# Storing the result of a decode kernel from ScalarE's DMA queue in place of SyncE's

## The chip, the cores and the metric

The kernel runs on one core of one Trainium2 chip. The metric is the device time of one execution in microseconds (us), and medians of several executions are quoted. The span of a profile is about 1.8 us shorter than the time on the clock, so spans are compared with spans and times with times. In the views of the profile SP is SyncE, PE TensorE, DVE VectorE, ACT ScalarE and POOL GpSimd; a q at the end of such a name marks what the engine's sequencer does, and L247 is line 247 of the kernel.

## The reference, cut to what matters

One token attends to a cache of 65,536 keys and values per head, is projected, and is mixed by a gate with the output of a small token MLP.

```python
def reference(A_x, A_k_cache, A_v_cache, A_wq, A_wo, B_x, B_w1, B_b1, B_w2, B_b2, gate_w):
    g = _sigmoid((x * gate_w).sum(-1, keepdims=True))
    # A: q = x @ wq; 16 query heads on 8 KV heads; Sk = 65536, Dh = 256
    #    softmax(q k^T * Dh**-0.5) @ v, then @ wo
    # B: layernorm, outer product with w1 + b1, gelu, sum over F with w2, + b2
    return g * a + (1 - g) * b        # shape (1, 1, 448), bf16
```

The two caches hold 2 x 8 x 65536 x 256 bf16 values, 537 MB. The result is 448 bf16 values, 896 bytes.

## The kernel before

SyncE issues all the large loads, in program order, each after a wait for its buffer to come free. At the end it also stores the result. ScalarE uses its own DMA queue for six small loads at the very start and then runs a loop of copies and exponentials.

```python
        @block.sync
        def _(eng):
            # ... wq loads ...
            for j in range(NP):                       # 32 blocks of keys and values
                last = j == NP - 1
                if j >= 1:
                    eng.wait_ge(sem_tr[NB - 1], BODY * (j - 1) + DC)   # TensorE has read the keys
                load(kring, A_k_cache, j, 0, HV if last else NV, HV * (j % 2), sem_k)
                # ...
                else:
                    eng.wait_ge(sem_pv, j)                             # TensorE has read the values
                load(vbuf, A_v_cache, j, 0, NLATE if last else NV, 0, sem_v)
                # ... the last block in pieces; wo_sb once per head ...
            eng.wait_ge(s_fin, 1)
            eng.dma_start(out_ap, out_g[0:P:P // NCG, :]).then_inc(sem_out, 16)
            eng.wait_ge(sem_out, 16)
```

The result lies in `out_g` in four partitions (0, 32, 64 and 96) of 112 values each. VectorE writes it as the last piece of work:

```python
            vec.wait_ge(s_proj, H)
            vec.scalar_tensor_tensor(out_g[:, :], prj[:, 0:WG], bcast[:, 0:1], run_g[:, :],
                                     op0=ALU.mult, op1=ALU.add).then_inc(s_fin, 1)
```

ScalarE's program ends with its loop:

```python
        @block.scalar
        def _(act):
            # ... six small loads, sqrt, exp ...
            with nc.Fori(0, NP, 1, engines=OrderedEngineSet([act.engine])) as j:
                # ... evacuations of transposed keys (ktT), exponentials (pT) ...
                with act.If(j < FT):
                    act.wait_ge(s_u, j + 1)
                    act.activation(z_b[:, :], z_b[:, :], AF.Tanh).then_inc(s_tanh, 1)
```

The softmax here doesn't subtract the row's maximum and nothing guards it: scores larger than these inputs give would overflow.

Of the kernel before, what the change touches and what calls it, by code (L numbers as in the profile page):

```python
# [12 lines left out]
def bass_gated_mix__gqa_block_cached__mixer_token_mlp__decode_kernel(  # L13
# [25 lines left out]
    P = 128  # L39
# [28 lines left out]
    NCG = 4  # L68
# [22 lines left out]
    with ctx:  # L91
        def sb(shape, dt, name):
            return ctx.enter_context(nc.sbuf_tensor(name, shape, dt))
# [4 lines left out]
        def new_sem(name):  # L98
            return ctx.enter_context(nc.semaphore(name))
# [56 lines left out]
        out_g = sb([P, WG], bf16, "out_g")  # L156
# [43 lines left out]
        s_fin = new_sem("s_fin")  # L200
        sem_out = new_sem("sem_out")
# [4 lines left out]
        out_ap = out.rearrange("a b (q n) -> (a b q) n", q=NCG)  # L206

        def src(cache, j, n0=0, n1=NV):
            g, m = divmod(j, PPH)
            s = cache[0, g, m * BODY * CH:(m + 1) * BODY * CH, :].rearrange("(p n) d -> p n d", p=P)  # L210
            return s[:, n0:n1, :].rearrange("p n d -> p (n d)")

        @block.sync
        def _(eng):
            eng.dma_start(wq_a.rearrange("p j n -> p (j n)"),  # L215
                          A_wq[0:WF * P, :].rearrange("(p j) n -> p (j n)", p=P)).then_inc(sem_wq, 16)
            eng.dma_start(wq_b, A_wq[WF * P:DM, :].rearrange("r (a n) -> (r a) n", a=2)  # L217
                          ).then_inc(sem_wq, 16)
            def load(dst, cache, j, n0, n1, at, sem):
                eng.dma_start(dst[:, at + n0:at + n1, :].rearrange("p n d -> p (n d)"), src(cache, j, n0, n1)  # L220
                              ).then_inc(sem, 16)

            for j in range(NP):
                last = j == NP - 1
                if j >= 1:
                    eng.wait_ge(sem_tr[NB - 1], BODY * (j - 1) + DC)
                load(kring, A_k_cache, j, 0, HV if last else NV, HV * (j % 2), sem_k)
                if last:
                    load(kring, A_k_cache, j, HV, NV, HV, sem_kb)
                if j == 0:  # L230
                    eng.wait_ge(s_q, 1)
                    eng.wait_ge(s_hb, 1)
                else:
                    eng.wait_ge(sem_pv, j)
                load(vbuf, A_v_cache, j, 0, NLATE if last else NV, 0, sem_v)
                if last:
                    for (n0, n1), sem in zip(pieces, sem_vp):
                        load(vbuf, A_v_cache, j, n0, n1, 0, sem)
                if j % PPH == 0:
                    g = j // PPH  # L240
                    if g >= 1:
                        eng.wait_ge(s_proj, g)
                    eng.dma_start(wo_sb[:, :, :],
                                  A_wo[g * REP * DH:(g + 1) * REP * DH, :].rearrange(
                                      "(h p j) n -> p h (j n)", h=REP, j=2)).then_inc(sem_wo, 16)
            eng.wait_ge(s_fin, 1)
            eng.dma_start(out_ap, out_g[0:P:P // NCG, :]).then_inc(sem_out, 16)  # L247
            eng.wait_ge(sem_out, 16)

        @block.gpsimd  # L250
        def _(eng):
# [10 lines left out]
        def _(pe):  # L262
# [74 lines left out]
            def piece_wait(n):  # L337
                for (n0, _), sem in zip(pieces, sem_vp):
                    if n == n0:
                        pe.wait_ge(sem, 16)  # L340
# [249 lines left out]
        @block.scalar  # L590
        def _(act):
            act.dma_start(xrow_b, x_row_ap).then_inc(sem_x, 16)
            act.dma_start(grow_b, gate_w.rearrange("(a n) -> a n", a=1)).then_inc(sem_misc, 16)
            for i, w in enumerate((B_w1.rearrange("a f -> (a f)"), B_b1, B_w2.rearrange("f a -> (f a)"))):
                act.dma_start(wrows_b[i * FT:(i + 1) * FT, :], w.rearrange("(k p) -> k p", p=P)
                              ).then_inc(sem_misc, 16)
            act.dma_start(b2_b[:, :], B_b2.rearrange("(a n) -> a n", a=1)).then_inc(sem_misc, 16)
            act.sem_inc(sem_exp, 2)
            for b in range(1, NB, 2):
                act.sem_inc(sem_ev[b], 1)  # L600
            act.wait_ge(s_d2a, 1)
            act.sqrt(statb[:, 3:4], statb[:, 2:3])
            act.activation(statb[:, 5:6], statb[:, 4:5], AF.Exp, scale=-1.0).then_inc(s_a2d, 1)

            pt_reg = act.alloc_register("pt_reg")
            act.reg_mov(pt_reg, DC)


            def weights(k, c):
                p0 = act.snap(pt_reg, min_val=0, max_val=DC)  # L610
                act.wait_ge(sem_qk, c + 3)
                act.activation(pT[:, bass.ds(p0 + k % DC, 1), :].rearrange("p o n -> p (o n)"),  # L612
                               sps[:, k % 2, 0:2 * NT], AF.Exp, scale=scale).then_inc(sem_exp, 1)
                if k == DC - 1:
                    act.reg_sub(pt_reg, DC, pt_reg)

            with nc.Fori(0, NP, 1, engines=OrderedEngineSet([act.engine])) as j:
                c0 = act.snap(j * BODY, min_val=0, max_val=NC)
                for k in range(BODY):
                    act.wait_ge(sem_qk, c0 + (k + 1))  # L620
                    for b in range(1, NB, 2):
                        act.wait_ge(sem_tr[b], c0 + (k + 1))
                        act.activation(ktT[:, k % KTB, b, :], kst_b[:, b, :], AF.Copy).then_inc(sem_ev[b], 1)  # L623
                    if k >= 1:
                        weights(k - 1, c0 + (k - 1))
                weights(BODY - 1, c0 + (BODY - 1))
                with act.If(j < FT):
                    act.wait_ge(s_u, j + 1)
                    act.activation(z_b[:, :], z_b[:, :], AF.Tanh).then_inc(s_tanh, 1)  # L629


# [26 lines left out]
```

## Time and profile before

| | before |
|---|---|
| time, median of the first 3 runs (range) | 1270.92 us (1270.15 to 1271.19) |
| span of the profile | 1268.1 us |
| bytes moved, mean rate | 544.39 MB, 429 GB/s |
| chain that ended last | DMA 68%, PE 31%, all else rounds to 0% |
| start of `out_g` to the end of the span | 2.41 us, 0.19% of the span |

The chain that ended last is the work that the profile follows back from the last instruction, at each step to what released it. The page of the kernel before has these lines on DMA and on this chain. In the queue lines, q1 is SyncE's queue, q10 is ScalarE's, and q8 and q14 fetch instructions; the columns are packets, megabytes and the share of the engines' time.

```profile
DMA packets 12366, 544.39 MB, mean 429 GB/s; under 512 B 1345, under 2 KB 3395, under 8 KB 3779
q1 hardware_dynamic: 12264, 544.22, 99.4%
q10 hardware_dynamic: 90, 0.01, 0.0%
DMA 68%; PE 31%; issue 0%; SPq 0%; DVE 0%; ACT 0%; ACTq 0%
```

The kernel is a stream of cache reads. SyncE's queue moves practically every byte, and its issuing engine rounds to 0% of the chain. What SyncE itself waits for is shown by the view of the waits of the DMA queue's own engine (waiter, releaser: us in total, times, longest):

```profile
SPq L220 <- PE kst L277: 646.5, 31, 25.2
SPq L220 <- PE acc L327: 530.2, 31, 24.4
SPq L247 <- DVE out_g L587: 31.5, 1, 31.5
SPq L91 <- DMA out_dram<-out_g: 1.0, 1, 1.0
```

SyncE waits nearly all the time for TensorE to give buffers back. Before the store (line 247) it has waited 31.5 us for VectorE, so no cache load is left for it to issue. After the store it waits 1.0 us for the data to land. That the last loads have also landed is shown by the view by windows of the 4.08 us before the store (start:end and length in us, then busy us of PE, PEld, which is TensorE's loading of weights, DVE, ACT and POOL, granted TensorE clock, DMA share, GB/s):

```profile
1261.98:1266.06 4.08, 2.59 (x86) 2.36 (x84) 1.30 (x5) 0.00 (x0) 0.00 (x0) 0.96 0.01 4
```

At 4 GB/s, against a mean of 429, no stream of loads is left for the store to queue behind.

The timeline of the end of the kernel before (start us, duration us, engine, line, operation, and in brackets the idle time before it and who ended it):

```profile
1264.97 0.16 DVE L545 TENSOR_TENSOR oTn<-sps,rden 128x4 bf16<-128x4 f32 x1 [1.96 <-PE sps L347]
1265.70 0.33 DVE L587 SCALAR_TENSOR_TENSOR out_g<-prj,bcast,run_g 128x112 bf16<-128x112 f32 x1 [0.57 <-PE prj L367]
1266.06 0.65 SPq L247 DMA_DIRECT2D out_dram<-out_g  x1
```

And the closing instructions of every engine, which share the line number 91 (engine, operation, count: duration in ns min/median/max, first and last start us):

```profile
L91 ACTq DRAIN  x1: 8/8/8, 1257.1 to 1257.1; - x1
L91 SPq COMPARE_BRANCH  x1: 33/33/33, 1267.7 to 1267.7; - x1
L91 SPq DRAIN  x1: 7/7/7, 1267.9 to 1267.9; - x1
L91 PEldq EVENT_SEMAPHORE  x1: 51/51/51, 1268.1 to 1268.1; - x1
```

ScalarE has nothing to do from 1257.1 us on. The store takes 0.65 us on SyncE's sequencer, and SyncE goes on (COMPARE_BRANCH) at 1267.7, when the data has landed. The 0.65 us alone would mislead: the Trainium skill, "Perfetto Trace Analysis", section "Summary: the profiler window per engine type", says that the record of such a DMA ends with the issue and leaves out the movement of the data. This trace agrees: the store was issued in 0.65 us, and SyncE was released 1.02 us after that record ended.

### The profile page before, as it was taken

How to read it: one execution, taken by the hardware profiler on the slowest of the kernel's cores; microseconds unless marked ns; L12 is line 12 of the kernel's file. 1: busy time of each engine (PE TensorE's matmuls, PEld its weight loads, DVE VectorE, ACT ScalarE, POOL GpSimd, SP SyncE). 2: the span in 40 equal slices, each digit the busy share in tenths (PEclk: the TensorE clock that was granted, in tenths of full speed). 3: DMA queues.
4: the chain of work that ended last, by engine and by line, in shares of the span. 5: the costliest groups of instructions: out<-in, count | busy, mean ns of one | idle time of the engine just before them, and what ended most of it. 6: DMA issues, size and time to landing. Idle time of an engine off the chain costs nothing.

```text
span 1268.1 us, 38721 instructions
## 1 busy us (share of the span) xinstructions
PE 912.6 (72%) x17053; PEld 860.7 (68%) x17055; DVE 417.9 (33%) x741; ACT 537.2 (42%) x786; POOL 0.9 (0%) x7
## 2 busy tenths in 40 slices
PE   1886668766778666697665876767867678766698
PEld 1776667766678666687665876657866568765687
DVE  2433334333344333343222332223332223331233
ACT  0543345543355433455333553334543245532355
POOL 0000000000000000000000000000000000000000
PEclk9988789788898788888788988789887788887889
DMA  9999999999999999999999999999999999999997
GB/s 411 424 428 438 432 432 428 438 436 430 436 426 438 434 430 440 426 436 432 432 440 426 436 430 436 436 428 434 430 440 432 430 432 430 442 432 430 430 424 323
DMA packets 12366, 544.39 MB, mean 429 GB/s; under 512 B 1345, under 2 KB 3395, under 8 KB 3779
## 3 DMA queue, kind: packets, MB, share of 16 engines
q1 hardware_dynamic: 12264, 544.22, 99.4%
q8 instruction: 8, 0.13, 0.0%
q10 hardware_dynamic: 90, 0.01, 0.0%
q14 instruction: 4, 0.02, 0.0%
HBM read 544.22 MB, written 0.00 MB: 429 GB/s over the span
## 4 chain that ended last, share of the span: by engine, by line
DMA 68%; PE 31%; issue 0%; SPq 0%; DVE 0%; ACT 0%; ACTq 0%
DMA kring<-in_A_k_cache_dram 68%; PE kst L277 25%; PE sps L297 5%; PE acc L327 1%; PE kst L313 0%; PE sps L347 0%; PE acc L319 0%; PE sps L354 0%; ACT pT L612 0%; SPq L217 0%; PE prj L367 0%; SPq L215 0%; DVE out_g L587 0%; DVE oTn L545 0%; ACTq L612 0%
## 5 line engine op out<-in xcount | busy, mean ns | idle before, releaser
L277 PE MATMUL kst<-ident,kring 128*128 128x128 f32 x4096 | 561.5, 298 | 314.7 <-DMA kring<-in_A_k_cache_dram 313.6
L623 ACT ACTIVATE ktT<-kst 128x1024 bf16<-128x1024 bf16 x512 | 499.5, 1021 | 671.2 <-PE kst L277 670.9
L277 PEld LDWEIGHTS kst<-ident,kring 128*128 128x128 f32 x4096 | 511.9, 155 | 324.3 <-issue 321.6
L529 DVE COPY ktT<-kst 128x1024 bf16<-128x1024 bf16 x512 | 354.1, 692 | 775.4 <-PE kst L277 751.9
L297 PEld LDWEIGHTS sps<-qcur,ktT 128*128 128x128 bf16 x8192 | 237.8, 96 | 4.6 <-issue 2.1
L297 PE MATMUL sps<-qcur,ktT 128*128 128x2 bf16 x8192 | 236.6, 163 | 1.9 <-issue 1.9
L327 PE MATMUL acc<-vbuf,pT 128*2 128x256 bf16 x4064 | 142.8, 309 | 3.1 <-issue 3.1
L327 PEld LDWEIGHTS acc<-vbuf,pT 128*2 128x2 bf16 x4064 | 104.8, 94 | 33.1 <-issue 3.9
L612 ACT ACTIVATE pT<-sps 128x32 f32 x256 | 51.8, 202 | 17.0 <-PE sps L297 17.0
L319 PE MATMUL acc<-pT,ones_sq 128*128 128x32 bf16 x256 | 11.7, 178 | 12.7 <-ACT pT L612 12.7
L319 PEld LDWEIGHTS acc<-pT,ones_sq 128*128 128x128 bf16 x256 | 8.6, 97 | 15.4 <-ACT pT L612 15.4
L629 ACT ACTIVATE z_b<-z_b 128x448 bf16<-128x448 bf16 x14 | 8.1, 577 | 20.4 <-DVE z_b L516 20.4
L534 DVE COPY accs<-acc 128x288 f32<-128x288 f32 x8 | 3.7, 458 | 37.9 <-PE acc L327 37.9
L381 PE MATMUL acc<-vbuf 42*128 42x42 bf16 x1 | 0.2, 215 | 8.5 <-DMA b_b<-in_B_b_dram 8.5
L381 PEld LDWEIGHTS acc<-vbuf 42*128 42x128 bf16 x1 | 0.1, 99 | 8.6 <-DMA b_b<-in_B_b_dram 8.6
L510 DVE TENSOR_TENSOR z_b<-wtmp,u_b 128x448 bf16<-128x448 bf16 x14 | 5.5, 393 | 1.0
L522 DVE TENSOR_TENSOR gu<-wtmp,z_b 128x448 bf16<-128x448 bf16 x14 | 5.5, 392 | 1.0
L520 DVE TENSOR_SCALAR z_b<-z_b 128x448 bf16<-128x448 bf16 x14 | 3.9, 277 | 5.9 <-ACT z_b L629 5.9
L508 DVE TENSOR_TENSOR wtmp<-u_b 128x448 bf16<-128x448 bf16 x14 | 5.5, 392 | 1.0
L514 DVE TENSOR_TENSOR z_b<-u_b,wtmp 128x448 bf16<-128x448 bf16 x14 | 5.5, 392 | 1.0
L504 DVE TENSOR_SCALAR wtmp<-hbT,params 128x448 bf16<-128x448 bf16 x14 | 4.7, 337 | 2.6 <-issue 2.6
L506 DVE TENSOR_SCALAR u_b<-wtmp,params 128x448 bf16<-128x448 bf16 x14 | 4.7, 337 | 2.6 <-issue 2.6
(84 smaller groups left out, 80.5 us busy)
## 6 DMA issues: line engine op xcount, KB each, us to landing
kring<-in_A_k_cache_dram SPq DMA_DIRECT2D x2, 4096.0 KB, 22.8
vbuf<-in_A_v_cache_dram SPq DMA_DIRECT2D x1, 6144.0 KB, 24.4
wo_sb<-in_A_wo_dram SPq DMA_DIRECT2D x8, 448.0 KB, 28.6
vbuf<-in_A_wq_dram SPq DMA_DIRECT2D x1, 3072.0 KB, 10.3
vbuf<-in_A_v_cache_dram SPq DMA_DIRECT2D x1, 1024.0 KB, 26.5
vbuf<-in_A_v_cache_dram SPq DMA_DIRECT2D x1, 768.0 KB, 27.5
vbuf<-in_A_wq_dram SPq DMA_DIRECT2D x1, 512.0 KB, 11.1
kring<-in_A_k_cache_dram SPq DMA_DIRECT2D x31, 27.8
```

The costliest lines, as they stand in the source:

```text
L277: ins = pe.transpose(kst[:, b, i * P:(i + 1) * P], kring_f[:, at + NT * (k % DC) + 4 * b + i, :], ident[:, :])
L297: ins = pe.matmul(sps[:, par, 2 * nt:2 * nt + 2], ktT[:, par, b, ntl * DH + dj:(ntl + 1) * DH:2], qcur[:, dj, :], start=(dj == 0), stop=(d ...
L319: pe.matmul(acc[:, DENC:SELC], ones_sq[:, :], pT[:, r, :], start=False, stop=(r == BODY - 1), skip_group_check=True)
L327: ins = pe.matmul(acc[o:o + REP, 0:DH], pT[:, r, 2 * nt:2 * nt + 2], vbuf[:, n, :], start=False, stop=False, skip_group_check=True)
L508: vec.tensor_tensor(W, U, U, op=ALU.mult)
L510: vec.tensor_tensor(Z, W, U, op=ALU.mult)
L514: vec.tensor_tensor(Z, U, W, op=ALU.add)
L522: vec.tensor_tensor(gu[:, :], W, Z, op=ALU.mult).then_inc(s_pb, 1)
L529: vec.tensor_copy(ktT[:, k % KTB, b, :], kst_b[:, b, :]).then_inc(sem_ev[b], 1)
L612: act.activation(pT[:, bass.ds(p0 + k % DC, 1), :].rearrange("p o n -> p (o n)"), sps[:, k % 2, 0:2 * NT], AF.Exp, scale=scale).then_inc(s ...
L623: act.activation(ktT[:, k % KTB, b, :], kst_b[:, b, :], AF.Copy).then_inc(sem_ev[b], 1)
L629: act.activation(z_b[:, :], z_b[:, :], AF.Tanh).then_inc(s_tanh, 1)
```

## The change: intent and diff

The store is issued by ScalarE, which has been idle for 9 us, rather than by SyncE, which has carried all the loads. The thought behind it is that a store on another queue can't be held up by the stream of loads.

```diff
@@ SyncE, after the loop of loads
-            eng.wait_ge(s_fin, 1)
-            eng.dma_start(out_ap, out_g[0:P:P // NCG, :]).then_inc(sem_out, 16)
-            eng.wait_ge(sem_out, 16)
@@ ScalarE, after its loop
                     act.activation(z_b[:, :], z_b[:, :], AF.Tanh).then_inc(s_tanh, 1)
+            act.wait_ge(s_fin, 1)
+            act.dma_start(out_ap, out_g[0:P:P // NCG, :]).then_inc(sem_out, 16)
+            act.wait_ge(sem_out, 16)
```

## The prediction

> **What bounds the kernel now.** It streams two caches: the page's DMA row reads 544.39 MB at a mean of 429 GB/s, and queue 1 (SyncE's) has 99.4% of the engines' time. The chain that ended last is 68% DMA (loads of `kring`) and 31% PE; SyncE's queue, VectorE and ScalarE round to 0%. SyncE's own waits are 646.5 us for TensorE to free `kring` and 530.2 us for it to free `vbuf`. A 0.9 KB store cannot change that stream.
>
> **The one stage touched** is the tail, from the timeline. VectorE starts `out_g` at 1265.70 us and takes 0.33 us. SyncE issues the store at 1266.06 (0.65 us), then waits 1.0 us for its completion, branches at 1267.7, and the closing semaphores end at 1268.1. So issue plus completion is about 1.65 us of 1268.1, 0.13%, all on the critical path.
>
> **What the change removes, adds and moves.** The listing of instruction order shows one DMA copy fewer on SyncE and one more at ScalarE's end, nothing else but line numbers. The store still waits for the same VectorE semaphore, then for its own completion.
> - No queueing is saved: SyncE's last cache loads are issued by 1234.6, and the last 4.1 us before the issue moved 4 GB/s (windows view).
> - ScalarE is free: its last activation ends at 1257.03, about 9 us before the store, so an instruction after its loop delays none of its work.
> - Issue on ScalarE: its small loads at the start took 0.21 to 0.53 us each, against 0.33 to 0.44 us for SyncE's cache loads. These overlap. My estimate from them is 0.65 us, give or take 0.2.
> - Completion: the Trainium skill, "DMA: Bandwidth & Descriptors", section "Issuing engines are not separate DMA queues", says that DMAs of either engine run on the same 16 DMA engines. So I keep 1.0 us. This trace, with its single store, cannot confirm it.
> - End: ScalarE in place of SyncE comes last to the closing barrier; their drains take 8 and 7 ns. No difference.
> - Early: ScalarE's six small loads already go through its queue (queue 10, 90 packets); the store is 1,250 us later.
>
> The sum is 0.0 us, give or take 0.3. The run-to-run range before is 1.04 us, so the change should not be visible in the time.
>
> **Prediction: 1270.9 us, 8 times in 10 between 1268.8 and 1273.0.** The range is mostly the spread between occasions, not the change. Chances: faster by over 2% 0.005, within 2% 0.99, slower by over 2% 0.005.
>
> **What would show each step right or wrong.** At the end of the timeline ScalarE's queue issues the store within 0.1 us of the end of `out_g`, for 0.45 to 0.85 us, and the last semaphore comes 1.9 to 2.3 us after that issue starts. The queue table gives queue 1 eight packets fewer (four data, four semaphores) and queue 10 eight more, 98. Bytes, GB/s and the chain's shares stay within a per cent. SyncE reaches its closing drain about 31 us earlier, and nobody profits.
>
> **What would make it wrong.** An instruction fetch after ScalarE's loop that takes longer than the 9 us of slack; a slow first use of ScalarE's queue after a millisecond of idleness; a completion from this queue that takes microseconds; or loops shifted in instruction memory so that PE or ScalarE slows in every pass, which the unchanged order makes unlikely. Any but the last costs single microseconds, far below the 25 us that 2% would take.

## The result, and the profile after

| | before | after |
|---|---|---|
| time, median of 6 runs each (range) | 1270.95 us (1270.09 to 1271.19) | 1271.14 us (1270.13 to 1271.51) |
| ratio, 95% interval | | 1.0002 (0.9989 to 1.0015) |
| span of the profile, granted clock | 1268.1 us, 0.847 | 1269.3 us, 0.842 |
| start of `out_g` to the end of the span | 2.41 us | 2.44 us |

Ratios here and below are the mean time of one kernel's fast runs over that of the other's of the same rounds, so they are not quite the ratio of the medians.

The time is the same. The page of the kernel after, same lines as before:

```profile
DMA packets 12365, 544.39 MB, mean 429 GB/s; under 512 B 1344, under 2 KB 3394, under 8 KB 3778
q1 hardware_dynamic: 12256, 544.22, 99.3%
q10 hardware_dynamic: 98, 0.01, 0.0%
DMA 68%; PE 31%; issue 0%; SPq 0%; DVE 0%; ACT 0%; ACTq 0%
```

Eight packets have moved from q1 to q10, and nothing else has: these are the four rows of the store and their four semaphore writes. The timeline of the end and the closing instructions of the kernel after:

```profile
1266.14 0.16 DVE L542 TENSOR_TENSOR oTn<-sps,rden 128x4 bf16<-128x4 f32 x1 [2.01 <-PE sps L344]
1266.87 0.33 DVE L584 SCALAR_TENSOR_TENSOR out_g<-prj,bcast,run_g 128x112 bf16<-128x112 f32 x1 [0.57 <-PE prj L364]
1267.23 0.62 ACTq L628 DMA_DIRECT2D out_dram<-out_g  x1
```

```profile
L91 SPq DRAIN  x1: 116/116/116, 1234.1 to 1234.1; - x1
L91 ACTq COMPARE_BRANCH  x1: 38/38/38, 1268.9 to 1268.9; - x1
L91 ACTq DRAIN  x1: 8/8/8, 1269.1 to 1269.1; - x1
L91 PEldq EVENT_SEMAPHORE  x1: 51/51/51, 1269.3 to 1269.3; - x1
```

SyncE now drains at 1234.1 us, 33.8 us earlier than before, and no one gains by it: its wait in the closing barrier is 35.0 us. The same steps follow with a different engine. Read from the trace's records to the nanosecond, they are:

| us | before (SyncE) | after (ScalarE) |
|---|---|---|
| end of `out_g` to start of the issue | 0.029 | 0.032 |
| issue | 0.652 | 0.618 |
| end of the issue to the branch after the wait | 1.016 | 1.068 |
| branch to the end of the span | 0.377 | 0.390 |
| `out_g` itself | 0.333 | 0.333 |
| sum | 2.407 | 2.441 |

In these two profiles the stage is 0.034 us longer after the change. The profile after is nevertheless 1.2 us longer, and it is worth seeing that this doesn't come from the store. The view by windows was asked for the stretch from the end of the last exponential to the start of `out_g`, in three parts (columns as above). Before:

```profile
1257.03:1259.30 2.27, 2.08 (x19) 1.07 (x24) 0.00 (x0) 0.00 (x0) 0.00 (x0) 1.00 0.99 411
1259.30:1261.98 2.68, 2.68 (x96) 2.05 (x88) 0.00 (x0) 0.00 (x0) 0.00 (x0) 1.00 0.50 196
1261.98:1265.70 3.72, 2.59 (x86) 2.36 (x84) 0.97 (x4) 0.00 (x0) 0.00 (x0) 1.00 0.02 4
```

After:

```profile
1256.51:1259.70 3.19, 3.14 (x20) 1.15 (x20) 0.00 (x0) 0.00 (x0) 0.00 (x0) 0.67 0.99 405
1259.70:1263.15 3.45, 3.39 (x97) 2.30 (x96) 0.00 (x0) 0.00 (x0) 0.00 (x0) 0.81 0.19 74
1263.15:1266.87 3.72, 2.59 (x84) 2.36 (x84) 0.98 (x5) 0.00 (x0) 0.00 (x0) 1.00 0.02 4
```

In the first two parts the same TensorE work took 6.64 us in place of 4.95 us at a granted clock of 0.67 and 0.81 in place of 1.00. This 1.69 us lies ahead of the store, in instructions that the change does not touch, and the third part, up to `out_g`, is 3.72 us in both. The end of the last exponential even came 0.52 us earlier in the profile after (1256.51 against 1257.03). That the issuer of the store does not cause it is seen in the kept traces of all runs: from the end of the last exponential to VectorE's copy of `acc`, this stretch took 5.01 us in five of the 13 profiles and 6.64 to 6.70 us in the other eight, and each of the two occurred with the store on SyncE (5.01 in `before`, 6.70 in `sp_chain32`), on ScalarE (5.01 in `act_chain32`, 6.65 in `after`) and on GpSimd (5.01 in `pool_chain32`, 6.65 in `pool_store`).

### The profile page after: what moved, and what is told of

It reads as the page before. It is cut to its first block, busy times and chain, and to the rows that moved or that the text cites. A ratio compares the mean times of both kernels' runs of the same rounds, so it can differ in the third digit from the quotient of the medians.

```text
span 1269.3 us, 38723 instructions
## 1 busy us (share of the span) xinstructions
PE 916.3 (72%) x17055; PEld 860.3 (68%) x17055; DVE 418.1 (33%) x741; ACT 536.8 (42%) x786; POOL 0.9 (0%) x7
## 4 chain that ended last, share of the span: by engine, by line
DMA 68%; PE 31%; issue 0%; SPq 0%; DVE 0%; ACT 0%; ACTq 0%
DMA kring<-in_A_k_cache_dram 68%; PE kst L274 25%; PE sps L294 5%; PE acc L324 1%; PE kst L310 0%; PE sps L344 0%; PE acc L316 0%; PE sps L351 0%; SPq L217 0%; ACT pT L609 0%; PE prj L364 0%; SPq L215 0%; DVE out_g L584 0%; DVE oTn L542 0%; ACTq L609 0%
## 5 line engine op out<-in xcount | busy, mean ns | idle before, releaser
L620 ACT ACTIVATE ktT<-kst 128x1024 bf16<-128x1024 bf16 x512 | 499.1, 1021 | 670.1 <-PE kst L274 669.7
L324 PE MATMUL acc<-vbuf,pT 128*2 128x256 bf16 x4064 | 147.8, 316 | 2.9 <-issue 2.9
L324 PEld LDWEIGHTS acc<-vbuf,pT 128*2 128x2 bf16 x4064 | 107.4, 96 | 35.7 <-issue 4.0
L310 PE MATMUL kst<-ktT,ones_sq 128*128 128x512 bf16 x22 | 6.1, 434 | 0.0
L364 PE MATMUL prj<-wo_sb,oTn 128*1 128x112 bf16 x128 | 3.3, 211 | 3.3 <-DVE oTn L542 3.3
```

Of the source, the lines that this page charges most:

```text
L310: pe.matmul(kst[:, NB - 1, :], ones_sq[:, :], ktT[:, KTB - 1, 0, 0:512], start=True, stop=True)
L324: ins = pe.matmul(acc[o:o + REP, 0:DH], pT[:, r, 2 * nt:2 * nt + 2], vbuf[:, n, :], start=False, stop=False, skip_group_check=True)
L620: act.activation(ktT[:, k % KTB, b, :], kst_b[:, b, :], AF.Copy).then_inc(sem_ev[b], 1)
```

## The experiments

The theory (A) is this: the store is on the critical path, but it costs the same from ScalarE's queue as from SyncE's, because no load stands ahead of it and ScalarE is idle. The rivals are: the queues do differ by some tenths of a us or more, and noise hid it (B); the end of the program hides the store, so that nothing done to it would show (C); any engine would do (D, a stronger form of A). Eleven experiments were run, all with correct results. The kernel before ran beside each of them (9 runs in the first group, median 1270.62 us; 7 in the second, 1270.74 us; 7 in the third, 1270.89 us).

### after_again: the change alone, five rounds

No edit.

> The changed kernel, unaltered, in five rounds for a narrower interval. Theory A (the store costs the same from either queue): ratio to the kernel before 1.000, within 0.0008 of it, that is under 1 us. Rival B (ScalarE's store is really slower or faster by some us and noise hid it): a ratio away from 1 by over 0.001, with an interval that leaves 1 out.

Measured: 1270.86 us (1270.54 to 1273.22) against 1270.62 us; ratio 1.0005, interval 0.9992 to 1.0019. The interval contains 1. But it spans 2.7 parts in a thousand, 3.4 us, so timing alone can't tell a difference under about 1.7 us, half of that interval, and the expectation was finer than the method: one of the five runs took 1273.22 us. Its profile repeats the stage: 2.434 us from the start of `out_g` to the end of the span, where the first profile of the change had 2.441. Hence the next pair, which multiplies the cost in question.

### sp_chain32 and act_chain32: the store 32 times over

Each kernel stores the same bytes 32 times, and each store waits for the one before. Shown for SyncE; in act_chain32 the same lines stand at ScalarE's end.

```diff
             eng.wait_ge(s_fin, 1)
-            eng.dma_start(out_ap, out_g[0:P:P // NCG, :]).then_inc(sem_out, 16)
-            eng.wait_ge(sem_out, 16)
+            for i in range(32):
+                eng.dma_start(out_ap, out_g[0:P:P // NCG, :]).then_inc(sem_out, 16)
+                eng.wait_ge(sem_out, 16 * (i + 1))
```

> SyncE stores the same result 32 times, each waiting for the one before: the cost of one store in this place, enlarged 31 times. From the one store before (0.65 us issue and 1.0 us completion) each further store should cost about 1.65 us, so 31 x 1.65 = 51 us more, about 1322 us. If the store were not on the critical path at all, or its cost were hidden in the end of the program, the time would grow by less than 40 us.

> ScalarE stores the same result 32 times, each waiting for the one before. Theory A: the time of the same chain on SyncE within 31 x 0.1 = 3 us, about 1322 us. Rival B (one queue costs more per store): a difference of 31 times whatever one store differs by, so 6 us or more for 0.2 us.

Measured: SyncE 1319.33 us (1318.49 to 1319.65), ratio 1.0381 (1.0367 to 1.0395); ScalarE 1319.76 us (1319.71 to 1320.43), ratio 1.0387 (1.0372 to 1.0401). The first line below is from the profile of the chain on SyncE (the line of the store: durations in ns min/median/max, first and last start us):

```profile
L248 SPq DMA_DIRECT2D out_dram<-out_g x32: 497/497/646, 1266.7 to 1315.0; - x32
```

The same view of the chain on ScalarE:

```profile
L629 ACTq DMA_DIRECT2D out_dram<-out_g x32: 520/520/612, 1267.3 to 1316.5; - x32
```

From the first start to the last, one store and its wait took 1.558 us on SyncE and 1.586 us on ScalarE (starts of the first and the 32nd record, over 31). The whole chain on ScalarE is 0.92 us longer from `out_g` to the end of the span; the mean times differ by 0.88 us. So ScalarE is dearer by about 0.03 us per store, the same 0.03 us that the single store showed. This figure rests on the traces. The times agree with it but are coarser: the slowest run of SyncE's chain (1319.65 us) is only 0.06 us under the fastest of ScalarE's (1319.71 us), and the intervals of the two ratios overlap. Rival B falls at any size that matters. Rival C falls too: 31 more stores lengthened the kernel by 48.7 us (medians), which is 31 x 1.57 where the trace has 31 x 1.558, so the store and its wait pass into the time in full. The view of the critical chain could not show this: in the kernel before, its list ends with `out_g` and leaves out the store. The expectation of 51 us was a little high: only the first issue took 0.646 us, the others took 0.497 us.

### pool_store and pool_chain32: GpSimd as a third issuer

The three lines of the store, and then the 32 stores, stand at the end of GpSimd's program, which before ends with its memsets at the start.

```diff
             eng.memset(ones_sq[:, :], 1.0).then_inc(sem_ident, 1)
+            eng.wait_ge(s_fin, 1)
+            eng.dma_start(out_ap, out_g[0:P:P // NCG, :]).then_inc(sem_out, 16)
+            eng.wait_ge(sem_out, 16)
```

> The one store issued from GpSimd in place of SyncE. If it does not matter at all which engine issues a 0.9 KB store (a stronger form of theory A), the ratio is 1.000 within 0.001. If what makes SyncE and ScalarE equal is that both have the same kind of queue, the end of the kernel from the end of out_g to the last semaphore should be longer than the 2.0 us of before, by an estimated 0.5 to 3 us.

> 32 stores one after the other from GpSimd. The single store from there showed an end of 2.87 us from the start of out_g to the last semaphore, 0.43 to 0.46 us more than from the other two, which the timing could not see. If that is real and comes with every store, the chain costs 1.8 to 2.1 us per store where SyncE's took 1.56 and ScalarE's 1.59, so 1326 to 1336 us. If it is a cost of the first store or chance, the chain costs 1.5 to 1.65 us per store, 1317 to 1322 us.

Measured: the single store 1271.31 us (1270.22 to 1271.80), ratio 1.0003 (0.9990 to 1.0017), so timing sees nothing, and by the ratio alone the stronger form of A would stand. Its profile shows 2.87 us from the start of `out_g` to the end of the span in place of 2.41: the issue started 0.296 us after `out_g` ended in place of 0.029, and the closing steps took 0.510 us in place of 0.377. The 0.46 us more lie just under the expected 0.5 to 3 us, an estimate that did not say where it came from. The wait between the end of the issue and the branch was 1.054 us, as for the other two (1.016 and 1.068), so the difference is in when GpSimd starts and how it closes, not in the completion. The chain settles that it is real: 1331.98 us (1330.76 to 1334.54), ratio 1.0488 (1.0471 to 1.0506), 61 us more than before where SyncE's chain was 49 us more. The waits of GpSimd in the chain (waiter, releaser: us, times, longest) and the line of the store (as above, durations in ns):

```profile
POOL out_dram L259 <- DMA out_dram<-out_g: 41.0, 31, 1.4
L259 POOL DMA_DIRECT2D out_dram<-out_g x32: 566/566/682, 1266.2 to 1324.8; - x32
```

A store and its wait took 1.89 us (starts of the first and the 32nd record, over 31) against 1.56 and 1.59 us. Dividing the 61 us by 31 would have given 1.97: the closing drain took 2.674 us here and 0.135 us after the single store, and that is no part of the repeated step. The Trainium skill, "DMA: Bandwidth & Descriptors", section "Anatomy of one DMA — SWDGE (gpsimd) path", gives about 2.0 us of fixed cost per DMA on GpSimd's path; the 1.89 us here, issue and wait together, are close to it. So rival D falls by 0.3 to 0.5 us per store. It is not true that the issuer doesn't matter; SyncE and ScalarE are equal to 0.03 us.

### act_busy10 and act_busy40: is ScalarE really free?

Useless copies were put on ScalarE between its loop and the store, 10 and 40 of them.

```diff
+            for _ in range(10):                       # 40 in act_busy40
+                act.activation(z_b[:, :], hbT[:, :], AF.Copy)
+                act.drain()
             act.wait_ge(s_fin, 1)
             act.dma_start(out_ap, out_g[0:P:P // NCG, :]).then_inc(sem_out, 16)
             act.wait_ge(sem_out, 16)
```

> ScalarE does 10 useless copies of 128x448 (each followed by a drain) after its loop and ahead of the store: an estimated 6 to 8 us of work, less than the 9 us for which ScalarE had nothing to do there. Theory A (slack): ratio to the kernel before within 0.001 of 1. If an instruction on ScalarE ahead of the store costs its own time, 6 to 8 us more.

> The same with 40 useless copies: 24 to 32 us of work, beyond the slack of about 9 us. Theory A: the store now waits for ScalarE and the kernel is longer by that work less the slack, 15 to 23 us. If the store could pass ScalarE's work, the time would grow by about 2 us less, since only the end of the work and no store would follow it.

Measured: with 10 copies 1270.39 us (1270.00 to 1270.62), ratio 0.9997 (0.9981 to 1.0014); with 40 copies 1286.23 us (1286.18 to 1286.29), ratio 1.0123 (1.0106 to 1.0140). The timeline of ScalarE with 10 copies, and VectorE's `out_g` from the same profile:

```profile
1256.13 6.38 ACT L628 ACTIVATE z_b<-hbT 128x448 bf16<-128x448 bf16 x10
1266.37 0.33 DVE L584 SCALAR_TENSOR_TENSOR out_g<-prj,bcast,run_g 128x112 bf16<-128x112 f32 x1 [0.57 <-PE prj L364]
1266.74 0.61 ACTq L631 DMA_DIRECT2D out_dram<-out_g  x1
```

With 40 copies:

```profile
1256.62 25.68 ACT L628 ACTIVATE z_b<-hbT 128x448 bf16<-128x448 bf16 x40
1266.85 0.34 DVE L584 SCALAR_TENSOR_TENSOR out_g<-prj,bcast,run_g 128x112 bf16<-128x112 f32 x1 [0.57 <-PE prj L364]
1282.36 0.61 ACTq L631 DMA_DIRECT2D out_dram<-out_g  x1
```

Ten copies end at 1262.51 us, and the store still starts 0.03 us after `out_g`: 6.4 us of work cost nothing. Forty end at 1282.30 us, and the store starts right behind them, 15.2 us after `out_g`; the kernel is 15.5 us longer. So the slack is real and has an end. ScalarE could take the store at no cost because its loop ends about 10 us before the result is ready; on the same queue, behind 40 copies, the store came late. Whether the store on SyncE would have saved 2 us beside 40 copies was not run.

### sp_behind_load and act_beside_load: a load in the way

The intent of the change would hold if a load stood ahead of the store. These kernels make such a case: SyncE issues a useless load of 8 MB 0.9 us before the store. In the first the store follows on SyncE's queue; in the second it is on ScalarE's.

```diff
+            eng.wait_ge(s_oTn, H)
+            load(kring, A_k_cache, 0, 0, NV, 0, sem_dum)     # 8 MB, rows of 64 KB
             # sp_behind_load: the store follows here; act_beside_load: it is at ScalarE's end
+            eng.wait_ge(sem_dum, 16)
```

> SyncE issues a useless load of 8 MB into the free key buffer when the last oTn is written, about 1 us before the result is ready, and then the store behind it on the same queue; the program ends when both have landed. This makes the case in which moving the store could matter. If the queue's order counts, the store lands only when the load has drained, about 19 us after its issue (8.4 MB at 430 GB/s), against 1.0 us before. Time about 1270.9 + 18 = 1289 us.

> The same useless load on SyncE's queue, but the store from ScalarE's. If queues are served in turn, the store lands within about 1.5 to 6 us of its issue while the load is still running for over 10 us, so much earlier than behind the load on SyncE's own queue. If all goes in one line whatever the queue, it lands no earlier than there. The time of the program is that of the load in both, about 1289 us.

Measured: 1290.38 us (1289.60 to 1291.00), ratio 1.0154 (1.0137 to 1.0171), and 1290.35 us (1289.82 to 1290.62), ratio 1.0156 (1.0139 to 1.0173). The two are alike, about 20 us above the kernel before: the program waits for the load either way. The profiles differ. The store and the branch behind its wait, with the store on SyncE's queue:

```profile
1267.73 0.65 SPq L250 DMA_DIRECT2D out_dram<-out_g  x1
L91 SPq COMPARE_BRANCH  x1: 33/33/33, 1288.8 to 1288.8; - x1
```

With the store on ScalarE's queue:

```profile
1266.50 0.62 ACTq L632 DMA_DIRECT2D out_dram<-out_g  x1
L91 ACTq COMPARE_BRANCH  x1: 38/38/38, 1275.2 to 1275.2; - x1
L91 SPq COMPARE_BRANCH  x1: 33/33/33, 1287.5 to 1287.5; - x1
```

In the first kernel the branch also waits for the load, so the store is read from the packet records: its four rows went out 20.1 to 20.6 us after the start of its issue, when the last packet of the load ended at 20.6. In the second ScalarE went on 8.7 us after the start of the issue, 12.3 us before SyncE, whose load was still running. So a second queue does let a store overtake a load. It does not make it quick: 8.7 us is more than the 1.5 to 6 us expected. The packet records suggest a reason: the load's packets of 64 KB take 2.4 us each, the store's rows went out at 5.6 to 5.9 us after the start of the issue, where they go out at 1.26 to 1.32 us with no load (kernel after), and their semaphore writes came another 2.43 us later, one such packet's time.

### act_beside_small and sp_behind_small: the same load in rows of 2 KB

```diff
-            load(kring, A_k_cache, 0, 0, NV, 0, sem_dum)
+            eng.dma_start(kring[:, 0:NV, :].rearrange("p (b a) d -> p b (a d)", a=4),
+                          A_k_cache[0, 0, 0:P * NV, :].rearrange("(b p a) d -> p b (a d)", p=P, a=4)
+                          ).then_inc(sem_dum, 16)
```

> As act_beside_load, but the useless 8 MB load is cut into rows of 2 KB in place of 64 KB. There the store from ScalarE's queue took 8.1 us after its issue to complete, and the records show it behind 64 KB packets of 2.4 us each, two or three per engine. If an engine changes queues only between packets, 2 KB packets make the store complete within 1 to 3 us after its issue. If the delay comes from the amount of data in flight and not from the packet size, it stays at 6 to 9 us.

> As sp_behind_load with rows of 2 KB: the store on SyncE's own queue, behind the load. If the queue's order counts whatever the packet size, the store completes only with the load's end, 18 us or more after its issue, and not within 3 us.

One look each, 1292.17 and 1292.62 us. The store on ScalarE's queue was done 5.4 us after the start of its issue (0.62 us of issue and 4.81 us more), which neither expectation held. The semaphore writes now followed their rows by 0.09 us in place of 2.43 us, so that part of the delay was the packet size. The rows themselves still went out only at 4.1 to 4.9 us in place of 5.6 to 5.9 us. The Trainium skill, "DMA: Bandwidth & Descriptors", section "Queues, rings and completion order", says that an engine changes queues only between packets. The gap before the semaphore writes agrees with that, if a row of the load is one packet: a row of 2 KB took 0.08 us, one of 64 KB 2.4 us. Of the time before the rows, 1.26 to 1.32 us are there without any load; the other 2.7 to 3.7 us are over 30 rows of 2 KB long, so waiting for one packet does not explain them, and no run here settles them.

With the store on SyncE's queue behind this load (the line of the store: duration in ns min/median/max):

```profile
L252 SPq DMA_DIRECT2D out_dram<-out_g x1: 13937/13937/13937, 1266.9 to 1266.9; - x1
```

The store's rows went out 22.5 to 22.8 us after the start of its issue, at the end of the load (23.0 us), as expected. The issue itself took 13.9 us in place of 0.65 us; that was not expected, and no run here shows its cause.

## Why the prediction was right, point by point

- The time (1270.9 predicted, range 1268.8 to 1273.0): 1271.14 us. "Within 2%" came true with a ratio of 1.0002. This was an easy hit: the range is wider than the whole 2.4 us of the stage, and GpSimd's dearer store (1271.31 us) fell inside it too. The account is borne out by the steps below, not by this number.
- "The sum is 0.0 us, give or take 0.3": +0.034 us in the touched stage by the profiles, and +0.03 us per store by the chains' traces. The 1.04 us of run-to-run range hid it, as said.
- "All on the critical path": shown by the chain on SyncE, where 31 more stores cost 31 x 1.57 us.
- "No queueing is saved": the first step is the same to 0.003 us, and the kernels with a useless load show what queueing would have looked like (20 us).
- "ScalarE is free": shown by 10 copies that cost nothing and 40 that cost 15.5 us.
- Issue on ScalarE 0.65 us, give or take 0.2: 0.618 us. The centre was a guess: the loads it was estimated from took 0.21 to 0.53 us, all less, and 0.65 was SyncE's own figure for the store. Completion kept at 1.0 us on the strength of the Trainium skill, "DMA: Bandwidth & Descriptors", section "Issuing engines are not separate DMA queues": 1.068 against 1.016 us, and 1.054 us from GpSimd, so the runs agree with it.
- The marks in the profile held: the store started 0.03 us after `out_g`, the last semaphore ended 2.08 us after the start of the issue, and eight packets changed queues. SyncE's drain came 33.8 us earlier where 31 was said; the 31 us was the wait until its store, not until its drain.
- None of the four dangers showed. The issue started 0.032 us after `out_g`, so no fetch of instructions outlasted the slack; the first use of the queue after a millisecond and the completion are inside the 2.08 us; and the passes did not slow: one copy of `ktT` on ScalarE took 1021 ns on average before and after, one matmul into `kst` on TensorE 298 and 297 ns.

No run was faster than either kernel clear of the noise, and none pointed to one that would be: the whole of `out_g`, store and closing is 2.4 us, 0.19% of the span.

## What to carry to other kernels

Before moving a DMA to another queue, look at what stands ahead of it on its present queue and how long the issuer has waited when it issues it: if the queue is empty and the wait is for data, the move is worth the difference of the two issuers, here 0.03 us. Where a load does stand ahead, another queue lets the store overtake it, but not for free (8.7 us beside 64 KB packets in place of 1.7). If a difference is far below the noise, repeat the operation in a chain that waits each time, and take the step from start to start in the trace; the time divided by the count can hold costs of the end as well (GpSimd's drain).

## What the Trainium skill lacked or had wrong

- "DMA: Bandwidth & Descriptors" gives a fixed cost for a DMA on GpSimd's path, but no figure for a small store with its wait per issuer: 1.56 us from SyncE, 1.59 us from ScalarE and 1.89 us from GpSimd, each in a chain of 32. The first issue of a chain is longer than the rest: 0.646 against 0.497 us on SyncE, 0.612 against 0.520 us on ScalarE, 0.682 against 0.566 us on GpSimd.
- The same page, section "Issuing engines are not separate DMA queues", calls the issue time "usually small relative to the DMA itself". For this store it was not: 0.65 us of the 1.67 us from the start of the issue to the branch on SyncE. Behind an 8 MB load in rows of 2 KB, the issue of a 0.9 KB store held SyncE for 13.9 us; behind the same bytes in rows of 64 KB it took 0.65 us.
- The same page, section "Queues, rings and completion order", gives the rule for changing queues but no delay. Beside a running load a store on the other queue was done after 8.7 us (rows of 64 KB) and 5.4 us (rows of 2 KB), against 1.7 us alone; with rows of 2 KB, each 0.08 us, the store's rows went out 2.7 to 3.7 us later than without a load, and this delay is open.
